# Padded column tables, whole-height spectral weight transfers, and one w2 block loaded earlier

## The chip, the cores and the metric

The kernel runs on one core of a Trainium2 chip. The core has a matrix engine (PE, with its weight loads listed as PEld), a vector engine (DVE), a scalar engine (ACT), GpSimd (POOL), a sync engine (SP) that here only issues transfers, and 16 DMA engines that move the data. The metric is the device time of one launch in microseconds; lower is better.

## The reference

One forward and backward pass of two blocks on an input of 2048 rows by 448 columns (bf16). Block A is a spectral filter: layer norm, a two-dimensional real FFT, a product with complex weights `w_r + i w_i` of shape 2048 x 225, the inverse FFT, and a residual. Block B is an MLP across the 2048 rows with a hidden width of 1792, after two layer norms, and another residual.

```python
def _A_ref(x, w_r, w_i):
    X = rfft2(x.astype(float32))
    X = X * (w_r + 1j * w_i)
    return irfft2(X, s=(S, D)).astype(bfloat16)

def _B_ref(x, w1, b1, w2, b2):
    h = _layernorm(x)
    u = gelu(einsum("bsd,sf->bdf", h, w1) + b1)
    return transpose(einsum("bdf,fs->bds", u, w2) + b2, 0, 2, 1)

h  = x + _A_ref(_layernorm(x), A_w_r, A_w_i)
h2 = h + _B_ref(_layernorm(h), B_w1, B_b1, B_w2, B_b2)
```

The outputs are `h2` and the gradients of x, w_r, w_i, w1, b1, w2 and b2 for a given `grad_out`.

## The kernel before

Everything is written as a list of operations which a planner (`Plan`, L141) puts in an order before the program is built. It holds a cost for each operation, a priority that follows the longest chain behind it, and rings of buffers; each engine then executes its own list strictly in that order. Transfers issued by SP keep the order in which the code names them (`place`, L471). Loads and tables go through SP (`ld` L482, `ld_parts` L547); stores go through POOL (`st` L488). A transfer that SP issues also waits until the one issued eight places earlier has landed, because the program gives SP's transfers eight semaphores in turn.

The FFT is done with matmuls. `fft_rows` (L704) folds the normed rows on DVE into the tile `w`, multiplies with the table `kf` into the bank kind `sp`, and evicts into `zt`. `fft_cols` (L743) takes 16 column steps. `step1` multiplies `zt` with the table `df`, which has 113 rows (DC), and DVE combines the two halves into `gg` (L766, two operations a step). `step2` multiplies `gg` with the table `hf` into `xs` (forward) or `ds` (backward). `cmul` (L800) is the complex product with the spectral weights on DVE: two products `t_r` and `t_i` (L809), then a sum and a difference (L816, L818), for five groups of column steps. Both L809 operations read the weights' tile as a whole, so they wait for both its parts. `ifft_cols` and `ifft_rows` go back with the tables `hi`, `di` and `kinv`.

The spectral weights are read twice from DRAM by `ld_w` (L563): into `w_t` for the forward pass and into `w_b` for the backward pass. SBUF partition 64 b + q holds the 16 weight rows from 32 q + 16 b on, 3,600 numbers or 7,200 bytes in one piece. `ld_w` moves each of the real and the imaginary part in two transfers, one for b = 0 and one for b = 1, of 64 partitions each.

The MLP's products fill the PE between these steps. `ps_mg` is grad_out times w2: 14 blocks of w2, each loaded with a transposing transfer by `ld_w2T` (L554) into the five-slot ring `w4`. `ps_mm` are the products with w1, w2 and later grad_out times g (gradient of w2), and `ps_mw` is the gradient of w1. The gradients of the spectral weights are five groups of DVE products into the tile `gw`, each stored by four POOL transfers of 64 partitions (L1222).

SP's order at the start is: the four parts of x, `kf`, the first w2 block and the two parts of `go_n` among them; then `df1`, `hf`, two w2 blocks, `w_t` in four transfers, `hi`, the fourth w2 block, `kinv`, `di0`, `ident`, `b1r`, `b2r`, and further w2 blocks. In the backward pass it is: the transposed grad_out (`goT`), `df0`, `w_b` in four transfers, `di1`, three parts of x again (`xr`), and the transposed `hlnT` and `du_t`.

Of the kernel before, what the change touches and what calls it, by code (L numbers as in the profile page):

```python
# [18 lines left out]
P = 128  # L19
S = 2048  # L20
D = 448
DF = 225
# [3 lines left out]
NJ = 16  # L26
DC = 113
# [10 lines left out]
def _tables():  # L38


    tb = {}
    q = np.arange(P)
    t_q, pl_q = q // 4, q % 4
    same = (pl_q[:, None] == np.arange(4)[None, :]).astype(np.float64)
    kf = np.zeros((P, 32, 4))
    ke = np.zeros((32, 4, P))
    ko = np.zeros((32, 4, P))
    for j in range(16):
        al = 2 * np.pi * (t_q * j % 32) / 32
        c, s = np.cos(al), np.sin(al) if j else -np.cos(np.pi * t_q)  # L50
        kf[:, 2 * j, :] = c[:, None] * same
        kf[:, 2 * j + 1, :] = -s[:, None] * same
        ke[2 * j] = c[None, :] * same.T
        ke[2 * j + 1] = -s[None, :] * same.T
        ko[2 * j] = -c[None, :] * same.T
        ko[2 * j + 1] = (-s if j else s)[None, :] * same.T
    tb["kf"] = _bf(kf.reshape(P, P))
    tb["kinv"] = _bf(np.stack([ke.reshape(P, P), ko.reshape(P, P), -ko.reshape(P, P)], 1))
    k2 = np.arange(DF)

    def dtab(scale):

        t = np.zeros((DC, 6, DC))
        ke_, ko_ = np.arange(0, DF, 2), np.arange(1, DF, 2)
        d = 112 - np.arange(DC)
        th = lambda k: 2 * np.pi * (d[:, None] * k[None, :] % D) / D
        twice = np.where(d == 112, 0.5, 1.0)[:, None]
        for i, (f, k) in enumerate(((np.cos, ke_), (np.cos, ko_), (np.sin, ke_), (np.sin, ko_))):
            t[:, i, 0:len(k)] = twice * f(th(k)) * scale[k]
        t[:, 4:6] = -t[:, 2:4]  # L70
        return t

    wt = np.full(DF, 2.0 / (S * D))
    wt[[0, DF - 1]] = 1.0 / (S * D)
    tb["df1"] = _bf(dtab(wt))
    tb["df0"] = _bf(dtab(np.ones(DF)))

    def itab(w):
        a = np.zeros((P, 2, DF))
        b = np.zeros((P, 2, DF))  # L80
        d = np.arange(DF)
        for c in range(2):
            kk = np.arange(P) + 97 * c
            th = 2 * np.pi * (kk[:, None] * d[None, :] % D) / D
            a[:, c] = np.cos(th) * w[kk][:, None]
            b[:, c] = np.sin(th) * w[kk][:, None]
        a[: 128 - 97, 1] = 0
        b[: 128 - 97, 1] = 0
        return np.stack([a, b], 1)

    tb["di0"] = _bf(itab(np.ones(DF)))
    wc = wt.copy()
    wc[0] = 0
    tb["di1"] = _bf(itab(wc))

    pp = np.arange(64)
    p = 16 * (pp % 4) + pp // 4
    qq = np.arange(64)
    hf = np.zeros((P, NJ + 1, 2, 2, 64))
    hi = np.zeros((P, NJ, 2, 64))  # L100
    lo, up = slice(0, 64), slice(64, 128)
    th = lambda r: 2 * np.pi * (p[:, None] * (32 * qq[None, :] + r) % S) / S
    for j in range(NJ):
        for b in range(2):
            hi[(lo, up)[b], j, 0], hi[(lo, up)[b], j, 1] = np.cos(th(j + 16 * b)).T, np.sin(th(j + 16 * b)).T
        if j:
            c, s = np.cos(th(j)), np.sin(th(j))
            hf[lo, j, 0, 0], hf[up, j, 0, 0], hf[lo, j, 0, 1], hf[up, j, 0, 1] = c, s, -s, c
            c, s = np.cos(th(32 - j)), np.sin(th(32 - j))
            hf[lo, j, 1, 0], hf[up, j, 1, 0], hf[lo, j, 1, 1], hf[up, j, 1, 1] = c, -s, -s, -c  # L110
    c, s = np.cos(th(0)), np.sin(th(0))
    hf[lo, 0, 0, 0], hf[lo, 0, 0, 1], hf[up, 16, 0, 0], hf[up, 16, 0, 1] = c, -s, s, c
    c, s = np.cos(th(16)), np.sin(th(16))
    hf[up, 0, 1, 0], hf[up, 0, 1, 1], hf[lo, 16, 1, 0], hf[lo, 16, 1, 1] = c, -s, -s, -c
    tb["hf"], tb["hi"] = _bf(hf), _bf(hi)
    tb["ident"] = _bf(np.eye(P))
    return tb
# [280 lines left out]
def kernel(  # L398
# [159 lines left out]
    def table(name, ringname, shape):  # L558
        t = const2(ringname, shape, name)
        ld(t, lambda b: b[:], hnd[name].ap(), int(np.prod(shape)) * 2)  # L560
        return t

    def ld_w(dst):  # L563
        for c, src in enumerate((A_w_r, A_w_i)):
            v = src.rearrange("(q b r) k -> b q r k", b=2, r=NJ)
            for b_ in range(2):
                ld_parts(dst, [(c, b_)], lambda b, c=c, b_=b_: b[64 * b_:64 * b_ + 64, c], v[b_], 64 * NJ * DF * 2)

    ld_x(0)
    kf = const("kf", [P, 5, P])  # L570
# [4 lines left out]
    ld_x(2)  # L575
    ld_go(8, 16)
    ld_x(3)
    df1 = table("df1", "df", [DC, 6, DC])
    hf = table("hf", "hf", [P, NJ + 1, 2, 2, 64])
    ld_w2T(1)  # L580
    ld_w2T(2)
    w_t = big(4, [P, 2, NJ, DF], "w_t")
    ld_w(w_t)
    hi = const("hi", [P, NJ, 3, 64])
    ld(hi, lambda b: b[:, :, 1:3, :], hnd["hi"].ap(), P * NJ * 2 * 64 * 2, w=(hi, 0))
    ld_w2T(3)
    kinv = table("kinv", "kinv", [P, 3, P])
    di0 = table("di0", "di", [P, 2, 2, DF])
    ident = table("ident", "ident", [P, P])
# [153 lines left out]
    def fft_cols(zt, dtab, dst):  # L743


        G = {}

        def step1(j):
            pr = bank("sp", [P, 4, DC])
            calls = []  # L750
            for k, c in ((0, 0), (1, 2), (2, 1), (3, 3)):
                for half, rows_ in ((0, LO), (1, UP)):
                    plane = 2 * j + (half if k < 2 else 1 - half)
                    t = k if k < 2 else k + 2 * half
                    calls.append((DC, lambda k=k, rows_=rows_, pr=pr: pr[rows_, k, :],
                                  lambda c=c, plane=plane: zt[:, c, plane, :], lambda t=t: dtab[:, t, :], True, True))
            matmuls(pr, calls, [zt, dtab], mm(*[DC] * 4), "cols")
            g_ = G[j] = k1([P, 2, 2 * DC], "gg")
            if j == 0:
                copy(evict(452), lambda: g_[:].rearrange("p s (k t) -> p s t k", t=2),  # L760
                     lambda: pr[:].rearrange("p (s t) k -> p s t k", t=2), [pr], [g_])
                return
            b = pl.buf("f2", [P, 2, DC], "gb", F32)
            copy(on_act(226), lambda: b[:], lambda: pr[:, 2:4, :], [pr], [b])
            for s_, op in ((0, ALU.add), (1, ALU.subtract)):
                pl.op(on_dve(226), lambda e, on, s_=s_, op=op: e.tensor_tensor(  # L766
                    out=g_[:, s_, :].rearrange("p (k t) -> p t k", t=2), in0=pr[:, 0:2, :], in1=b[:], op=op),
                    r=[pr, b], w=[(g_, s_)])

        def step2(j):  # L770
            px = bank("sp", [P, 2, DF])
            calls = []
            for im in range(2):
                if j == 0:
                    terms = [[(0, 0, 0), (0, 16, 1)], [(0, 0, 0), (0, 16, 1)]]
                else:
                    terms = [[(j, j, 0)], [(16 - j, 16 - j, 1)]]
                for n in range(len(terms[0])):
                    for half, rows_ in ((0, LO), (1, UP)):
                        gj, ti, s_ = terms[half][n]  # L780
                        calls.append((DF, lambda im=im, rows_=rows_, px=px: px[rows_, im, :],
                                      lambda ti=ti, half=half, im=im: hf[:, ti, half, im, :],
                                      lambda gj=gj, s_=s_: G[gj][:, s_, 0:DF], n == 0, n == len(terms[0]) - 1))
            rd = [G[0]] if j == 0 else [(G[j], 0), (G[16 - j], 1)]
            matmuls(px, calls, rd + [hf], mm(*[DF] * (len(calls) // 2)), "cols")
            copy(evict(450), lambda: dst[:, :, j, :], lambda: px[:], [px], [(dst, j)])

        step1(8)
        step2(8)
        for a in range(7, 0, -1):  # L790
            step1(a)
            step1(16 - a)
            step2(a)
            step2(16 - a)
        step1(0)
        step2(0)
# [354 lines left out]

    df0 = table("df0", "df", [DC, 6, DC])
    w_b = big(0, [P, 2, NJ, DF], "w_b")
    ld_w(w_b)
    di1 = table("di1", "di", [P, 2, 2, DF])
# [52 lines left out]
    for j0, j1 in JG:  # L1210
        cur = []

        def out(a, b, cur=cur):
            t = pl.buf("e4", [P, 2, b - a, DF], "gw")
            cur.append(t)
            return ((lambda: t[:, 0]), (lambda: t[:, 1])), lambda c: [(t, c)]

        cmul(ds, xs, out, j0, j1, True)
        t = cur[0]
        for c in range(2):  # L1220
            for b_ in range(2):
                st(o23[c][b_, :, j0:j1, :], lambda t=t, c=c, b_=b_: t[64 * b_:64 * b_ + 64, c],  # L1222
                   64 * (j1 - j0) * DF * 2, [(t, c)])

    LO, UP = slice(0, 64), slice(64, 128)
    last = None
# [73 lines left out]
```

## Time and profile before

| what | value |
|---|---|
| time, median of 3 runs | 363.59 us (363.09 to 381.46) |
| the profiled execution: its own time | 366.62 us |
| its span, first to last instruction | 364.8 us |
| PE busy | 333.0 us (91%) |
| DVE busy | 273.2 us (75%) |
| ACT busy | 192.5 us (53%) |
| POOL busy | 59.6 us (16%) |
| bytes moved by DMA | 80.67 MB, mean 221 GB/s |
| SP's DMA queue, share of 16 engines | 71.0% |

Times inside the profile count from the span's first instruction. "Busy" counts the time in which an engine executes; a wait's row names who waited, for what, how long in total, how many times, and the longest. A chain or timeline row gives the start, the length and the instruction. In the DMA views the window is cut in 40 equal slices: the row GB/s says what all engines together moved in each slice.

### The profile page before, as it was taken

The numbers are of one execution on the slowest core, as the hardware profiler recorded it, in microseconds if no ns is written. First come the engines' busy times: TensorE is split into PE (matmuls) and PEld (weight loads), VectorE is DVE, ScalarE is ACT, GpSimd is POOL, SyncE is SP. The second block draws the span as 40 slices with busy tenths as digits, with TensorE's granted clock in tenths as the row PEclk, the third lists the DMA queues.
The fourth block names the chain that finished last, engine by engine and source line by source line (L and its number), as shares of the span: only waits on it lengthen the run. The fifth ranks groups of instructions, "written<-read, shape, count | busy, mean of one in ns | idle before, by whom it ended". The sixth has DMA issues, their size and how long they took to land.

```text
span 364.8 us, 6559 instructions
## 1 busy us (share of the span) xinstructions
PE 333.0 (91%) x2411; PEld 180.7 (50%) x2411; DVE 273.2 (75%) x705; ACT 192.5 (53%) x387; POOL 59.6 (16%) x107
## 2 busy tenths in 40 slices
PE   0538799999999999999999999899999999999994
PEld 0224445577655555545555555555455765434441
DVE  5993869979738999252225978889999999977442
ACT  1372554438638777210237232589787899434332
POOL 0000000002210111032210200011111444545221
PEclk9976989999999999999999999999999999999999
DMA  7999997999899999299999999999996574554553
GB/s 173 329 145 223 197 183 154 268 203 239 265 318 275 326 263 305 98 291 292 198 280 235 249 230 204 215 109 215 205 190 221 175 246 174 202 203 179 212 203 152
DMA packets 138192, 80.67 MB, mean 221 GB/s; under 512 B 98318, under 2 KB 130928, under 8 KB 138032
## 3 DMA queue, kind: packets, MB, share of 16 engines
q1 hardware_dynamic: 130672, 52.67, 71.0%
q0 software_dynamic: 7488, 27.58, 21.5%
q8 instruction: 19, 0.31, 0.4%
q14 instruction: 13, 0.11, 0.1%
HBM read 30.12 MB, written 27.08 MB: 157 GB/s over the span
## 4 chain that ended last, share of the span: by engine, by line
PE 75%; DVE 9%; SPq 8%; DMA 4%; ACT 2%; issue 1%; POOLq 0%; ACTq 0%
PE ps_mm L505 40%; PE ps_sp L505 13%; PE ps_mw L505 12%; PE ps_mg L505 10%; SPq L482 7%; DMA w2T<-in_B_w_dram 4%; DVE junk L1126 2%; DVE junk L1110 2%; SPq L547 2%; DVE w L719 1%; ACT v L1119 1%; DVE u L719 1%; DVE go_r L1129 1%; DVE w L497 0%; DVE nm L1116 0%
## 5 line engine op out<-in xcount | busy, mean ns | idle before, releaser
L505 PE MATMUL ps_mg<-go_n,w2T 128*128 128x448 bf16 x224 | 53.0, 374 | 19.9 <-DMA go_n<-in_grad_out_dram 13.3
L505 PE MATMUL ps_mm<-goT,g_t 128*128 128x512 bf16 x224 | 55.6, 380 | 0.5 <-ACT v L1119 0.5
L505 PE MATMUL ps_mw<-du_t,hlnT 128*128 128x448 bf16 (+1 forms) x256 | 44.9, 353 | 0.0
L505 PE MATMUL ps_mm<-gT,w2c 128*128 128x448 bf16 x224 | 42.9, 352 | 0.5 <-DVE gT L1008 0.5
L505 PE MATMUL ps_mm<-du,w1T 128*128 128x449 bf16 x224 | 43.1, 353 | 0.0
L505 PE MATMUL ps_mm<-hln,w1c 128*128 128x448 bf16 x224 | 42.7, 352 | 0.0
L505 PEld LDWEIGHTS <-w2T 128*128 128x128 bf16 x224 | 20.8, 101 | 38.9 <-DMA w2T<-in_B_w_dram 16.1
L495 ACT CAST s<-ps_mw 128x448 bf16<-128x448 f32 x36 | 18.0, 535 | 29.8 <-PE ps_mw L505 26.3
L505 PEld LDWEIGHTS <-hlnT 128*128 128x128 bf16 (+1 forms) x256 | 20.3, 97 | 24.5 <-issue 7.6
L505 PEld LDWEIGHTS <-w2c 128*128 128x128 bf16 x224 | 21.9, 98 | 21.1 <-issue 0.7
L505 PEld LDWEIGHTS <-w1T 128*128 128x128 bf16 x224 | 21.8, 97 | 21.1
L505 PEld LDWEIGHTS <-w1c 128*128 128x128 bf16 x224 | 21.9, 98 | 20.5
L505 PEld LDWEIGHTS <-g_t 128*128 128x128 bf16 x224 | 19.8, 97 | 21.0 <-issue 3.6
L497 DVE CAST s<-ps_mw 128x448 bf16<-128x448 f32 x28 | 17.1, 622 | 17.3 <-PE ps_mw L505 11.2
L1094 DVE SCALAR_TENSOR_TENSOR h<-ps_mm,b2c,hr 128x448 bf16<-128x448 f32 x16 | 9.9, 678 | 23.2 <-PE ps_mm L505 22.9
L488 POOL DMA_DIRECT2D out_dram<-s x30 | 16.4, 548 | 65.7 <-ACT s L495 36.3
L1119 ACT ACTIVATE v<-ps_mm,nm,rstd_h 128x448 f32<-128x448 f32 x16 | 11.6, 724 | 26.9 <-DVE nm L1116 24.5
L495 ACT CAST s<-ps_mm 128x512 bf16<-128x512 f32 x38 | 22.7, 600 | 4.7 <-PE ps_mm L505 4.4
L1101 ACT ACTIVATE gb2j<-go_r 128x448 bf16<-128x448 bf16 x16 | 9.2, 574 | 28.2 <-DMA go_r<-in_grad_out_dram 27.8
L766 DVE TENSOR_TENSOR gg<-ps_sp,gb 128x226 bf16<-128x226 f32 x60 | 20.6, 410 | 2.6 <-ACT gb L495 2.6
L495 ACT CAST eo<-ps_sp 128x450 bf16<-128x450 f32 x31 | 16.4, 554 | 5.1 <-PE ps_sp L505 5.1
L495 ACT CAST zt<-ps_sp 113x512 bf16<-113x512 f32 x27 | 13.8, 603 | 8.2 <-PE ps_sp L505 8.1
(122 smaller groups left out, 552.5 us busy)
## 6 DMA issues: line engine op xcount, KB each, us to landing
w2c<-in_B_w_dram SPq DMA_DIRECT2D x8, 896.0 KB, 8.3
out_dram<-s POOLq DMA_DIRECT2D x14, 512.0 KB, 3.9
out_dram<-s POOLq DMA_DIRECT2D x16, 448.0 KB, 2.8
w1c<-in_B_w_dram SPq DMA_DIRECT2D x6, 1024.0 KB, 10.7
x<-in_A_x_dram SPq DMA_DIRECT2D x4, 448.0 KB, 7.0
go_n<-in_grad_out_dram SPq DMA_DIRECT2D x2, 896.0 KB, 7.1
hn_d<-x POOLq DMA_DIRECT2D x4, 448.0 KB, 5.9
hln_d<-hln POOLq DMA_DIRECT2D x4, 448.0 KB, 4.2
```

Source lines behind the costliest of these rows:

```text
L482: e.dma_start(out=out(dst), in_=in_() if callable(in_) else in_, **kw)
L488: e.dma_start(out=out() if callable(out) else out, in_=in_())
L495: e.copy(out=out(), in_=in_())
L497: e.tensor_copy(out=out(), in_=in_())
L505: e.matmul(out(), lhsT=lhsT(), rhs=rhs(), start=start, stop=stop)
L547: e.dma_start(out=out(dst), in_=in_() if callable(in_) else in_, **kw)
L719: pl.op(tt(4 * n), lambda e, on: e.tensor_tensor(out=out(), in0=in0(), in1=in1(), op=op), r=r, w=w_)
L766: pl.op(on_dve(226), lambda e, on, s_=s_, op=op: e.tensor_tensor(out=g_[:, s_, :].rearrange("p (k t) -> p t k", t=2), in0=pr[:, 0:2, :], i ...
L1094: pl.op(on_dve(448), lambda e, on, t=t, p2=p2, h2=h2: e.scalar_tensor_tensor(out=h2[:], in0=p2[:, 0:D], scalar=b2c[:, t:t + 1], in1=hr[t / ...
L1101: pl.op([("ACT", 0.55, 0.65)], lambda e, on, h=h: e.activation(out=gb2j[:], in_=go_r[:, h, :], func=ACT.Copy, accum_out=gb2[:, h:h + 1]), ...
L1110: pl.op([("DVE", 0.69, 0.77)], lambda e, on: e.tensor_tensor_reduce(out=junk[:], in0=pb[:, 0:D], in1=xhat(), scale=nm.rneg[:, h:h + 1], sc ...
L1119: pl.op([("ACT", 0.6, 0.7)], lambda e, on: e.activation(out=v[:], in_=pb[:, 0:D], func=ACT.Identity, scale=nm.rstd[:, h:h + 1], bias=nm1[: ...
```

## The change

Four edits:

- The tables `df1` and `df0` get 128 rows in place of 113; the added rows are zeros and are not read, since the matmul takes rows 0 to 112.
- `ld_w` moves each part of the spectral weights in one transfer of 128 partitions. The DRAM side is written as `b q (r k)`: an outer index b of 2 (step 3,600 numbers), then q of 64 (step 7,200), then 3,600 numbers in one piece. The SBUF side has 128 partitions.
- The spectral gradients are stored in the same form: two POOL transfers a group in place of four, 10 in all in place of 20.
- The fourth w2 block is loaded ahead of `w_t` instead of behind `hi`.

```diff
     def dtab(scale):
-        t = np.zeros((DC, 6, DC))
+        t = np.zeros((P, 6, DC))
...
-            t[:, i, 0:len(k)] = twice * f(th(k)) * scale[k]
+            t[0:DC, i, 0:len(k)] = twice * f(th(k)) * scale[k]
...
     def ld_w(dst):
         for c, src in enumerate((A_w_r, A_w_i)):
-            v = src.rearrange("(q b r) k -> b q r k", b=2, r=NJ)
-            for b_ in range(2):
-                ld_parts(dst, [(c, b_)], lambda b, c=c, b_=b_: b[64 * b_:64 * b_ + 64, c], v[b_], 64 * NJ * DF * 2)
+            ld_parts(dst, [c], lambda b, c=c: b[:, c].rearrange("p r k -> p (r k)"),
+                     src.rearrange("(q b r) k -> b q (r k)", b=2, r=NJ), P * NJ * DF * 2)
...
-    df1 = table("df1", "df", [DC, 6, DC])
+    df1 = table("df1", "df", [P, 6, DC])
     hf = table("hf", "hf", [P, NJ + 1, 2, 2, 64])
     ld_w2T(1)
     ld_w2T(2)
+    ld_w2T(3)
     w_t = big(4, [P, 2, NJ, DF], "w_t")
     ld_w(w_t)
     hi = const("hi", [P, NJ, 3, 64])
     ld(hi, lambda b: b[:, :, 1:3, :], hnd["hi"].ap(), P * NJ * 2 * 64 * 2, w=(hi, 0))
-    ld_w2T(3)
...
-                                  lambda c=c, plane=plane: zt[:, c, plane, :], lambda t=t: dtab[:, t, :], True, True))
+                                  lambda c=c, plane=plane: zt[:, c, plane, :], lambda t=t: dtab[0:DC, t, :], True, True))
...
-    df0 = table("df0", "df", [DC, 6, DC])
+    df0 = table("df0", "df", [P, 6, DC])
...
         for c in range(2):
-            for b_ in range(2):
-                st(o23[c][b_, :, j0:j1, :], lambda t=t, c=c, b_=b_: t[64 * b_:64 * b_ + 64, c],
-                   64 * (j1 - j0) * DF * 2, [(t, c)])
+            st(o23[c][:, :, j0:j1, :].rearrange("b q r k -> b q (r k)"),
+               lambda t=t, c=c: t[:, c].rearrange("p r k -> p (r k)"), P * (j1 - j0) * DF * 2, [(t, c)])
```

The sizes given to the planner change with the transfers, so it also writes a somewhat different order for every engine. Around the first read of the weights, PE's new list takes up the fourth w2 block's product between the column steps, and DVE's new list has 17 `gg` operations ahead of the first `t_r` (12 before). In the backward pass the two orders are the same up to the first products with `w_b`.

## The prediction

> **What bounds the kernel now.** I read first the busy times by stage: from 46.4 us to 359 us PE has hardly an idle microsecond (64.40 of 64.40 in 246.6 to 311, 48.00 of 48.00 in 311 to 359), so any time that PE loses in the middle is lost for good. DVE is nearly full up to 311 as well:
>
> ```profile
> 246.60:311.00 64.40, 64.40 (x577) 36.95 (x572) 63.20 (x149) 56.55 (x112) 16.20 (x30) 1.00 0.87 205
> 311.00:359.00 48.00, 48.00 (x272) 21.33 (x271) 30.91 (x54) 18.09 (x37) 19.39 (x36) 1.00 0.53 194
> ```
>
> (Columns: stretch, length, busy us of PE, PEld, DVE, ACT, POOL, granted clock, DMA share, GB/s.) Idle PE time lies before 46.4. Who PE waits for in 0 to 60 us:
>
> ```profile
> PE ps_mg L505 <- DMA w2T<-in_B_w_dram: 6.6, 2, 3.5
> ```
>
> These are a wait of 3.5 us for the second w2 block (PE goes on at 29.15) and one of 3.1 us for the fourth (46.44). SP's list tells why:
>
> ```profile
> 10.53 5.55 SPq L482 DMA_DIRECT2D hf<-tab_hf  x1
> 16.12 12.55 SPq L482 DMA_TRANSPOSE w2T<-in_B_w_dram  x2
> 28.71 1.23 SPq L547 DMA_DIRECT2D w_t<-in_A_w_r_dram  x2
> ...
> 31.92 10.97 SPq L482 DMA_TRANSPOSE w2T<-in_B_w_dram  x1
> ```
>
> A transposing transfer behind copies sits in its issue until those have drained (10.97 us behind `w_t` and `hi`). What drains slowly the DMA view of 0 to 50 us shows, in slices of 1.25 us:
>
> ```profile
> GB/s 0 86 315 292 155 205 156 277 358 406 354 343 375 175 349 366 193 29 23 28 23 245 159 255 230 248 207 236 219 225 192 168 214 145 194 219 198 22 109 284
> ```
>
> In slices 17 to 20 (21.3 to 26.3 us) the 16 engines move 23 to 29 GB/s. Two views inside it say what that is:
>
> ```profile
> DMA packets 44, 0.05 MB, mean 25 GB/s; under 512 B 13, under 2 KB 44, under 8 KB 44
> ...
> DMA packets 7, 0.06 MB, mean 23 GB/s; under 512 B 0, under 2 KB 0, under 8 KB 0
> GB/s 0 0 0 0 0 131 0 0 0 0 131 0 0 0 0 131 0 0 0 0 131 0 0 0 0 131 0 0 0 0 131 0 0 0 0 131 0 0 0 0
> ```
>
> The first is 21.6 to 23.4: rows of `df1` (1,356 bytes), one after another. The other two are 23.45 to 26.1: rows of `hf` (8,704 bytes), one every five slices of 66 ns, 0.331 us each. So the 113-row table went through one DMA engine alone, and the `hf` rows of that engine queued behind it while the rest had nothing to do. Transfers with 128 or 64 rows do use all: `w_t` in four 64-row transfers ran at 213 GB/s:
>
> ```profile
> DMA packets 710, 1.92 MB, mean 213 GB/s; under 512 B 457, under 2 KB 457, under 8 KB 710
> ```
>
> **How I read that.** 113 is prime and got one engine; 64 and 128 got the full width. I take it that a transfer is shared out evenly by its outermost index, on as many engines as divide it. Then the padded table gains and the new read of the weights loses: its DRAM side now leads with b = 2. No row shows such a transfer; the bounds are one engine (as `df1`) and 16 (as `w_t`). I take two, nearest to the `df1` row, the only one with a leading count that 16 doesn't divide.
>
> The Trainium skill (DMA: Bandwidth & Descriptors, "Why a DMA increments its semaphore by 16 and not by 1") states such a rule: the largest number up to 16 that divides the slowest dimension over one on both sides. By that rule 113 rows get one engine, the trace agrees (23 GB/s), and 2 against 128 gets two; no run here shows the latter yet.
>
> **The sum, part by part.**
>
> *Padded tables.* The other engines were done with `hf` near 20.5 us (193 GB/s in the slice that ends at 21.3, 29 after it). With 128 rows `df1`'s 0.17 MB take some 0.5 us at 350 GB/s and `hf` ends near 20.9 in place of 26.1. The second w2 block comes 5.2 us earlier, at about 23.9, and PE, free of `kf` work at 25.64, doesn't wait: the 3.5 us go. The fourth block is issued right behind the third, so the 3.1 us go too: -6.6 us, if nothing else stopped PE. In the backward pass `df0` isn't waited for by PE now; its gain there is nothing.
>
> *First whole-height read, `w_t`.* SP issues it after three w2 blocks (issue 2.2 us each where nothing holds it): 21.2 + 2.2 + 2.2 = 25.6; it starts when they are through, about 27.5. Two engines carry 128 rows of 7,200 bytes each; by the `hf` row of one engine 7,200 / 8,704 x 0.331 = 0.274 us, so 35.1 us: done at 62.6, landed about 63.5. DVE wants it early: `t_r` stands behind 17 `gg` and ahead of the rest. Before:
>
> ```profile
> 41.54 1.08 DVE L809 TENSOR_TENSOR t_r<-xs,w_t 128x1800 bf16<-128x1800 bf16 x1
> 42.54 1.09 DVE L809 TENSOR_TENSOR t_i<-xs,w_t 128x1800 bf16<-128x1800 bf16 x1
> ```
>
> Queued behind `t_r` on DVE is the 18th `gg`. PE's `step2` of column step 4 needs it, and PE takes its list in order, so PE stops near 42.5 us with six matmuls of the fourth w2 block done, until 63.5 + 1.08 + 1.09 + 0.3 = 66.0. That is the state that PE has now at 48.5 (six such matmuls and the `hf` steps after them: 46.44 + 2.01). So **+17.5 us, in which the -6.6 is already spent**. PE's granted clock was 0.50 in 26.4 to 32.0, around its idle time; PE would come back at half clock for a little: +0.5. Further w2 blocks queue behind `w_t`, `hi`, `kinv`, `di0` (some 3 us), then 3 us from drain to landing (26.1 to 29.1 now): about 69, and PE gets to the fifth block after 71. Together **+18**.
>
> *Second read, `w_b`.* Times as now; all is shifted by the 18. It starts near 225.7 behind `goT`; 35.1 us on two engines end near 261, plus one or two stores of 512 KB on the same engines (1.2 us of each engine) and landing: about 263, and `xr` right behind it. DVE wants `xr` at 246.62 and `w_b` at
>
> ```profile
> 247.25 1.10 DVE L809 TENSOR_TENSOR t_r<-ds,w_b 128x1800 bf16<-128x1800 bf16 x1 [0.25 <-ACT ds L495]
> ```
>
> so DVE stands about 16.5 us. PE has cover until about 252 (22 matmuls with `goT`, whose banks DVE partly evicts) and then stands too. DVE is 98% busy from there to 311, so its delay isn't made up: **+16.5**. `hlnT` and `du_t` come later with it, but are wanted only at 311.
>
> *Stores.* POOL issues 10 transfers fewer (0.53 us each); POOL is idle more than half of that stage, so 0. On two engines a store of 173 KB takes 64 rows x 1,350 bytes at the `hf` rate, 3.3 us against 2.8 us to landing now; the tile is wanted again some 6 us later. Uncovered it would be 0 to 1 us a group; I take 0.
>
> Sum: 18 + 16.5 = +34.5 us. On the profiled execution's 366.62 that is 401; on the median of 363.59, **398 us**. A run within 2% (7.3 us) can't be told from no change.
>
> **The rivals.**
>
> *1, not slower: the read uses all 16 engines.* The point that decides is whether the SBUF side's 128 or the DRAM side's 2 sets the width. For it: every transfer of 128 partitions in the trace has full width; against it: none of them has a small outer index. Then `w_t` takes 16 rows an engine at 0.274 to 0.54 us, at most the 8.7 us of now (1.84 MB at 213 GB/s), and only the -6.6 is left: 357 us, 1.8% faster. The Trainium skill (same page, "Rules for kernel authors") recommends this outcome's form, one 128-partition transfer in place of two halves. Chance 0.11.
>
> *2, the read is slower still.* `w_t` rows now take about 0.54 us of an engine (256 rows in 8.7 us on 16). If that price belongs to the rows and not to the crowding of all engines on 64 partitions, or if one engine gets it all, a read takes 69 or 70 us: +34 or +35 twice, 466 to 468 us. Against it: a lone engine kept 0.331 us for longer rows. Chance 0.07.
>
> *3, the second stall is hidden.* If PE's `goT` products ran on without DVE, only the +18 counts: 382. Against it: fixed orders and DVE at 98%. Chance 0.12.
>
> **How the numbers follow.** The forecast, 385 to 420, has 0.70: its upper end takes a row at the `df1` rate (31 rows in 1.8 us, so 0.31 us for 7,200 bytes: +4.4 us a read), some 3 us more of half clock at each stall, and more stores beside the second read; its lower end, cover of 6 us for each stall. The range 376 to 424 takes in rival 3 and leaves out rivals 1 and 2 (0.18). Rival 1 lies at the edge of 2%: faster 0.05, same 0.06; slower 0.89.
>
> **What would show it.** Right: in the changed kernel's DMA view about 50 GB/s for some 35 us from 27 us on, and again in the backward pass; `t_r` on `w_t` near 63; PE idle from about 42 to 66 and again some 15 us before the first product with `w_b`; the second w2 block's product near 25.6 with no wait for it. Wrong: over 200 GB/s during `w_t` (rival 1), a load of 70 us (rival 2), or a PE that doesn't stand in the backward pass (rival 3). A `gg` or bank that PE needs sooner than I read in the order would lengthen the first stall by little, since its end is set by the load.

## The result, and the profile after

The changed kernel takes 1.175 times as long as before (95% interval 1.159 to 1.191), some 64 us more. The undisturbed runs, which alone enter the ratios, are 425.66 and 428.27 us, and the profiled execution is a disturbed one of 434.45 us (span 432.7), so its marks come a few us late (2 to 4 us for the second to fourth mark, against `e_inplace` below). The forecast was slower, 398 us; the range ended at 424.

The direction and both stalls came as foreseen; a third loss was not. The marks of the two traces show where the time went:

| mark | before | after | shift |
|---|---|---|---|
| first matmul with the second w2 block | 29.15 | 25.38 | -3.8 |
| PE: first product with `w1c` | 104.31 | 129.75 | +25.4 |
| PE: first product with `w1T` | 189.70 | 215.14 | +25.4 |
| PE: first gradient of w1 (`ps_mw`) | 311.39 | 358.51 | +47.1 |
| last PE instruction ends | 359.50 | 426.46 | +67.0 |

The forecast had +18 for the second and third mark and +34.5 for the last two. PE's waits of the whole span of the changed kernel (who waited for what: us in total, times, longest) name all three losses:

```profile
PE ps_sp L505 <- DVE gg L765: 25.0, 1, 25.0
PE ps_mm L505 <- ACT s L495: 18.2, 1, 18.2
PE ps_mg L505 <- DMA go_n<-in_grad_out_dram: 13.3, 2, 12.6
PE ps_mw L505 <- DVE s L497: 12.7, 4, 5.4
PE ps_sp L505 <- DVE w L497: 5.6, 3, 4.6
PE ps_mg L505 <- DMA w2T<-in_B_w_dram: 3.5, 1, 3.5
```

The third and fifth were there before. The first is the stall at the first read, the second the one at the second read, the fourth is new, and the last is a w2 block at 121.6 us.

**First read.** The DMA view of 0 to 50 us no longer has the slices of 23 to 29 GB/s near 21 to 26 us; from 28.75 us on it has slices of about 52 instead. The second line is the window 27 to 65.5 us:

```profile
GB/s 0 66 351 346 152 272 142 316 354 389 358 359 387 423 420 177 157 108 268 267 206 169 6 46 52 58 65 52 52 58 52 65 52 52 58 125 224 133 52 46
...
DMA packets 2230, 2.38 MB, mean 62 GB/s; under 512 B 1972, under 2 KB 1972, under 8 KB 2227
```

DVE's rows (start, length, idle time before; its L808 is L809 of the kernel before) show what this did:

```profile
48.76 1.10 DVE L808 TENSOR_TENSOR t_r<-xs,w_t 128x1800 bf16<-128x1800 bf16 x1 [9.22 <-DMA w_t<-in_A_w_r_dram]
66.16 1.10 DVE L808 TENSOR_TENSOR t_i<-xs,w_t 128x1800 bf16<-128x1800 bf16 x1 [16.31 <-DMA w_t<-in_A_w_i_dram]
```

The kernel's description above says that both operations wait for both parts. The rows say otherwise: `t_r` went as soon as the real part had landed. `t_i` had to wait for the imaginary part, and that sets the end.

**Second read.** DVE waits for `xr`, which SP had issued behind `w_b`; the weights themselves are there by then:

```profile
291.61 0.40 DVE L693 TENSOR_SCALAR xr<-xr,rstd_x,nb_x 128x448 bf16<-128x448 bf16 x1 [19.95 <-DMA xr<-in_A_x_dram]
291.92 1.09 DVE L808 TENSOR_TENSOR t_r<-ds,w_b 128x1800 bf16<-128x1800 bf16 x1
```

**The clock behind each stall.** The table of stretches (columns: stretch, length, busy us of PE, PEld, DVE, ACT, POOL, granted clock, DMA share, GB/s) has each stall and the time behind it, and then the last stage:

```profile
42.64:67.64 25.00, 0.00 (x0) 0.00 (x0) 2.58 (x4) 0.67 (x1) 0.00 (x0) 0.58 0.27 74
67.64:73.80 6.16, 6.16 (x48) 2.81 (x48) 4.25 (x9) 2.18 (x5) 0.00 (x0) 0.50 0.85 193
275.40:293.60 18.20, 0.00 (x0) 0.00 (x0) 1.99 (x3) 1.93 (x4) 0.00 (x0) 0.59 0.96 81
293.60:299.10 5.50, 5.50 (x20) 1.87 (x19) 5.21 (x13) 3.41 (x7) 0.53 (x1) 0.50 1.28 230
358.50:426.50 68.00, 55.20 (x271) 23.24 (x269) 29.75 (x53) 19.00 (x39) 18.93 (x29) 0.87 0.46 142
```

PE is busy behind both stalls, but for 6.16 and 5.50 us at half clock: about 3 us of work are lost each time. In the last stage, which had 48.00 of 48.00 us before, PE now stands 12.8 of 68.00 us. Its busy time there also grew, from 48.0 to 55.2 us, at a mean granted clock of 0.87 (1.00 before).

**Stores.** DVE's rows of the gradients' tile in that last stage, and below them how long its stores took (from the view of the tile):

```profile
371.93 0.52 DVE L815 TENSOR_TENSOR gw<-t_r,t_i 128x675 bf16<-128x675 bf16 x1 [5.58 <-DMA out_dram<-gw]
...
383.45 0.52 DVE L815 TENSOR_TENSOR gw<-t_r,t_i 128x675 bf16<-128x675 bf16 x1 [6.79 <-DMA out_dram<-gw]
...
396.09 0.52 DVE L815 TENSOR_TENSOR gw<-t_r,t_i 128x675 bf16<-128x675 bf16 x1 [8.44 <-DMA out_dram<-gw]
```

```profile
DMA to landing us min/median/max: 6.4/8.1/10.9
```

Before, landing took 2.0/2.6/4.6 us. Each group uses all three slots of the ring `e4` (`t_r`, `t_i`, `gw`), so the next group's `gw` cannot be written until the group before has landed: the groups come 11 to 13 us apart (5 to 7 before). The evictions of `ps_mw` that DVE has queued behind `gw` wait with it, and PE for their banks.

### The profile page after: what moved, and what is told of

It reads as the page before. It is cut to its first block, busy times and chain, and to the rows that moved or that the text cites. A ratio compares the mean times of both kernels' runs of the same rounds, so it can differ in the third digit from the quotient of the medians.

```text
span 432.7 us, 6538 instructions
## 1 busy us (share of the span) xinstructions
PE 346.4 (80%) x2411; PEld 184.8 (43%) x2411; DVE 271.1 (63%) x702; ACT 194.0 (45%) x390; POOL 57.4 (13%) x97
## 4 chain that ended last, share of the span: by engine, by line
PE 53%; DMA 25%; DVE 10%; SPq 6%; ACT 3%; issue 2%; POOL 0%; DVEq 0%; ACTq 0%
PE ps_mm L505 32%; PE ps_sp L505 10%; DMA w_t<-in_A_w_i_dram 9%; DMA out_dram<-gw 9%; PE ps_mg L505 8%; DMA xr<-in_A_x_dram 5%; SPq L482 5%; PE ps_mw L505 4%; DVE junk L1109 2%; DMA w2T<-in_B_w_dram 2%; DVE junk L1125 2%; ACT v L1118 1%; SPq L547 1%; DVE w L718 1%; DVE u L718 1%
## 5 line engine op out<-in xcount | busy, mean ns | idle before, releaser
L505 PE MATMUL ps_mm<-goT,g_t 128*128 128x512 bf16 x224 | 58.4, 393 | 18.2 <-ACT s L495 18.2
L505 PE MATMUL ps_mg<-go_n,w2T 128*128 128x448 bf16 x224 | 54.6, 386 | 17.1 <-DMA go_n<-in_grad_out_dram 13.3
L505 PE MATMUL ps_mw<-du_t,hlnT 128*128 128x448 bf16 (+1 forms) x256 | 52.1, 396 | 12.7 <-DVE s L497 12.7
L505 PE MATMUL ps_mm<-gT,w2c 128*128 128x448 bf16 x224 | 42.9, 352 | 0.5 <-DVE gT L1007 0.5
L505 PEld LDWEIGHTS <-hlnT 128*128 128x128 bf16 (+1 forms) x256 | 22.0, 105 | 42.7 <-issue 28.3
L495 ACT CAST s<-ps_mw 128x448 bf16<-128x448 f32 x35 | 17.5, 535 | 47.6 <-PE ps_mw L505 38.7
L505 PE MATMUL ps_sp<-gg,hf 128*64 128x225 bf16 x136 | 11.2, 274 | 25.0 <-DVE gg L765 25.0
L495 ACT CAST s<-ps_mm 128x512 bf16<-128x512 f32 x43 | 25.4, 594 | 9.4 <-PE ps_mm L505 9.2
L815 DVE TENSOR_TENSOR gw<-t_r,t_i 128x675 bf16<-128x675 bf16 (+1 forms) x5 | 2.7, 536 | 27.6 <-DMA out_dram<-gw 27.6
```

Of the source, the lines that this page charges most:

```text
L495: e.copy(out=out(), in_=in_())
L505: e.matmul(out(), lhsT=lhsT(), rhs=rhs(), start=start, stop=stop)
```

## The experiments

Ratios are to the kernel before, run beside each; times in the text are a ratio's excess times 364 us.

| kernel | ratio (95%) | us |
|---|---|---|
| changed kernel | 1.1751 (1.1593 to 1.1909) | +64 |
| e_oldstores | 1.1128 (1.1061 to 1.1195) | +41 |
| e_oldread | 1.0311 (1.0259 to 1.0364) | +11 |
| e_inplace | 1.1473 (1.1353 to 1.1593) | +54 |
| e_first | 1.0586 (1.0511 to 1.0662) | +21 |
| e_second | 1.0499 (1.0393 to 1.0606) | +18 |
| e_best | 0.9988 (0.9958 to 1.0017) | 0 |
| e_noearly | 0.9838 (0.9792 to 0.9884) | -6 |
| e_early | 1.0041 (0.9987 to 1.0094) | +1.5 |
| e_w2first | 0.9821 (0.9779 to 0.9862) | -6.5 |
| e_lead128 | 0.9948 (0.9912 to 0.9984) | -2 |
| e_lead84, one run | 376.77 us (before: 365.3) | +11 |
| e_div, one run | 361.13 us (before: 365.5) | -4 |

### Are the stores a loss of their own?

`e_oldstores` takes the changed kernel and puts the old stores back; `e_oldread` puts the old reads back and keeps the new stores.

```diff
 # e_oldstores
-            st(o23[c][:, :, j0:j1, :].rearrange("b q r k -> b q (r k)"), ...)
+            for b_ in range(2):
+                st(o23[c][b_, :, j0:j1, :], lambda t=t, c=c, b_=b_: t[64 * b_:64 * b_ + 64, c], ...)
 # e_oldread
-            ld_parts(dst, [c], lambda b, c=c: b[:, c].rearrange("p r k -> p (r k)"), ...)
+            v = src.rearrange("(q b r) k -> b q r k", b=2, r=NJ)
+            for b_ in range(2):
+                ld_parts(dst, [(c, b_)], lambda b, c=c, b_=b_: b[64 * b_:64 * b_ + 64, c], v[b_], ...)
```

> The changed kernel with the gradients stored in four half-height transfers a group again; reads and tables stay changed. Theory: the whole-height stores cost the last 20 us of the loss (the tile gw waits for its own slow store, 8.1 us to landing where it was 2.6), so the time falls from 427 to about 407, the landing is 2.5 to 3 us again, and PE's last stage (first gradient of w1 to the end) is as long as before the change, some 50 us. Rival, as the prediction had it: the stores cost nothing and the last stage is longer because the late reads push other work into it; then the time stays within 3 us of 427.

> The changed kernel with both reads of the weights in four half-height transfers again; tables, w2 block and whole-height stores stay changed. Theory: both PE stalls go (25 and 18 us with their half clock, 54 us with the 6.6 that the tables save), so 427 falls to about 373, that is 357 plus some 16 to 20 for the stores. Rival: the stores hurt only because everything behind the late second read comes bunched; then the time is near 357.

Measured: +41 and +11. The stores are worth 64 - 41 = 23 us beside the late reads, and the on-record "0" falls. In `e_oldstores` PE's last stage, from the first gradient of w1 to PE's end, takes 47.5 us, as expected (48.1 before, 67.9 in the changed kernel), and the gradients' stores land as they did before:

```profile
DMA to landing us min/median/max: 2.3/2.6/3.4
```

By themselves the stores cost 11. The changed kernel and `e_oldread` order DVE's list differently: in `e_oldread`, as before the change, the first group of gradients comes early (277.9 us), and only the other four follow one another, 10 to 11 us apart. DVE's waits for a store there:

```profile
DVE gw L816 <- DMA out_dram<-gw: 16.8, 3, 5.7
```

That is three waits, where the changed kernel, with all five groups in the last stage, has four and 27.6 us. So the rival of `e_oldread`, that the stores hurt only because work comes bunched behind the late read, holds for part of the price: 11 of the 23 us are there without it.

### What do slow stores hold up?

`e_inplace` keeps the changed kernel's slow stores, but the products are written over `xs`, so that no slot is waited for.

```diff
         def out(a, b):
-            t = pl.buf("e4", [P, 2, b - a, DF], "gw")
-            ...
+            return (((lambda: xs[:, 0, a:b, :]), (lambda: xs[:, 1, a:b, :])),
+                    lambda c: [(xs, j) for j in range(a, b)])
```

> The changed kernel, its slow whole-height stores kept, but the gradients are written over xs (no longer needed by then) in place of a tile of the three-slot ring e4, so that no product on DVE waits for a store. Theory: the whole price of the stores beside the late reads is this wait (DVE stood 27.6 us for stores, four times), so the time is that of the run with half-height stores, 406 to 409, with stores that still take 8 us to land. Rival: the slow stores hold up the end through the queue or POOL's longer issue (0.83 us in place of 0.53); then the time stays above 420.

Measured: +54, between the two theories. The slot's wait is worth some 10 of the 23 us. PE's last stage is 55.7 us here, against 67.9 in the changed kernel and 47.5 in `e_oldstores`. What is left shows in this kernel's waits of 350 to 420 us:

```profile
ACT s L495 <- DMA out_dram<-s: 18.4, 5, 7.0
...
DVE s L497 <- DMA out_dram<-s: 14.8, 4, 6.3
...
PE ps_mw L505 <- ACT s L495: 4.5, 3, 3.4
```

The evictions now wait for the stores of the w1 gradient, and PE for their banks; behind the longest of these waits (378.7 to 390.6 us) its granted clock is 0.86. A store of `s` with 448 KB lands after 6.2 us (median; 2.8 in `e_oldstores`), the gradients' own with 168.8 KB after 13.5:

```profile
out_dram<-s POOLq DMA_DIRECT2D x16, 448.0 KB, 6.2
...
out_dram<-xs POOLq DMA_DIRECT2D x8, 168.8 KB, 13.5
```

Which engines the stores share shows in the trace's semaphore events: a store's semaphore gets 16 increments. In the changed kernel, of the store that POOL issues at 374.30 us, 14 come after 2.5 to 2.9 us and two later, at 380.79 and 382.05. So two engines carry its data. Of the group's second store, issued at 375.14, 12 come after 3.4 to 4.7 us, two at 381.17 and 382.41, right behind the first store's two, and the last two at 382.93 and 383.33. So the second store is on two other engines; the four other groups look the same. A store is 32 packets of 5,400 bytes at 0.223 us (median), 3.6 us on two engines. The rest of its landing is not the time of its data: in `e_lead128` (below) a store of the same size goes to 16 engines, and lands after 2.9 us all the same.

```profile
DMA to landing us min/median/max: 2.7/2.9/3.1
```

The stores of `s` behind the gradients are late in two ways. Of the one issued at 400.86 us, 14 increments come after 4.9 to 5.7 us and the last two after 7.5 and 8.2; in `e_oldstores` all 16 of the one issued at 381.48 come after 2.6 to 2.8. That the last two wait behind the gradients' rows is how I read it. Why the other 14 are late as well the trace doesn't show.

### What sets the width of a transfer?

`e_lead128` keeps one transfer a part for reads and stores, but lets the DRAM side lead with 128. `e_lead84` has old stores, and reads that lead with 8 (first) and 4 (second). `e_div` is the kernel before with tables of 116 (forward) and 120 rows (backward).

```diff
 # e_lead128, in ld_w (the stores likewise)
-                     src.rearrange("(q b r) k -> b q (r k)", b=2, r=NJ), P * NJ * DF * 2)
+                     src.rearrange("(p r) k -> p (r k)", r=NJ), P * NJ * DF * 2)
 # e_lead84
+                     src.rearrange("(q b r) k -> b q (r k)", b=lead, r=NJ), P * NJ * DF * 2)
+    ld_w(w_t, 8)
+    ld_w(w_b, 4)
 # e_div
-    df1 = table("df1", "df", [DC, 6, DC])
+    df1 = table("df1", "df", [116, 6, DC])
-    df0 = table("df0", "df", [DC, 6, DC])
+    df0 = table("df0", "df", [120, 6, DC])
```

> The changed kernel, reads and stores still whole-height in one transfer each, but the DRAM side leads with an index of 128 (the rows of the weights and of their gradients are then taken and put in another order, so the weights' rows stand against other rows of the spectrum; the work is the same). Theory: the leading 2 alone made them slow; with 128 a read takes 9 to 10 us on 16 engines at 200 GB/s or more, a store lands in 2 to 3 us, and the time is that of the tables and the w2 block alone, about 357. Rival: one transfer of 128 rows of 7,200 bytes is slow by itself (long rows, or one semaphore count): then a read takes 35 us again and the time stays near 427.

> Padded tables and earlier w2 block, half-height stores; both reads in one transfer a part, the DRAM side led by an index of 8 in the first read and of 4 in the second (the weights' rows then stand against other rows of the spectrum; the work is the same). Theory, as many engines as divide the leading number: 8 engines, 32 rows each at 0.274 us, some 9 us and 210 GB/s for the first; 4 engines, 64 rows each, 17.5 us and 105 GB/s for the second. So the first read costs little or nothing and the second a few us at most: 364 to 369. Rival, a leading index that is not 128 falls to two engines whatever it is: 35 us each, and about 409 as with both reads whole-height.

> The kernel before with 116 rows in the forward table (df1) and 120 in the backward one (df0) in place of 113; added rows are zeros. Theory, the largest number up to 16 that divides the rows: 4 engines for 116, 15 for 120. So 29 rows of 60 to 120 ns stand one after another on each of 4 engines, df1 is through 1.7 to 3.5 us after its start (7.2 with 113 rows, 2.2 with 128) and the last rows of hf end by about 22 us (26.1 with 113, 20.3 with 128); df0 is through in about 1 us if nothing else is on the engines. Rival, only numbers that 16 divides are shared out: then 116 behaves as 113, over 7 us, and hf ends at 26.

Both kernels with other leading indices, `e_lead128` and `e_lead84`, take the weights' rows in another order, so they do not compute the reference; the transfers have the same size and the work is the same.

The trace's semaphore events count the engines. The semaphore of a narrow transfer makes one jump near its issue (none where 16 increments follow), and later single increments as the data lands:

| transfer | leading counts (DRAM, SBUF) | late increments | median us of a 7,200-byte row | all 256 rows, us |
|---|---|---|---|---|
| `df1` before | 113, 113 | 1 | | |
| `df1` in e_div | 116, 116 | 4 | | |
| `df0` in e_div | 120, 120 | 15 | | |
| `w_t` after | 2, 128 | 2 | 0.274 | 38.7 |
| `w_b` in e_lead84 | 4, 128 | 4 | 0.334 | 27.3 |
| `w_t` in e_lead84 | 8, 128 | 8 | 0.548 | 19.0 |
| `w_t` in e_lead128 | 128, 128 | 16 | 0.273 | 6.0 |
| `w_t` before, four transfers | 64, 64 | 16 each | 0.534 | 9.1 |

So the leading 2 alone made the read slow: with 128 in front the same transfer takes 6.0 us, the stores land after 2.9 us, and the whole kernel is 2 us under the one before (357 us was expected). The DMA view of 26.7 to 32.8 us in `e_lead128`:

```profile
DMA packets 1187, 2.08 MB, mean 341 GB/s; under 512 B 930, under 2 KB 930, under 8 KB 1186
```

`e_div` agrees: `df1` is through 3.8 us after its first row, and `hf`'s last row ends at 22.4 us (26.1 before), a little over what was expected. `hf`'s rows cost 0.46 us there (median; 0.33 before).

The Trainium skill (DMA: Bandwidth & Descriptors, "Why a DMA increments its semaphore by 16 and not by 1") says that k engines are used, the largest number up to 16 that divides the slowest dimension of both sides, and that the semaphore jumps to 16 - k at once. Every row of the table agrees.

The number of engines is not the whole price. Eight engines took 19 us where 9 were expected, since a row cost 0.548 us in place of 0.274. The second read, on four, took 27.3 us where 17.5 were expected. PE stands 6.2 us at the first and 6.0 us at the second, and the time is 377 us instead of 364 to 369. The four half-height transfers of the kernel before pay the same double price on 16 engines. The Trainium skill has a rule for the latter (SBUF — State Buffer, "Door 1: The DMA port swizzle (why `[64,N]` ≈ `[32,N]`)"): 64 consecutive partitions reach only half of SBUF's ports. The measured 0.534 against 0.273 us agrees. By the same map, partitions 32 apart share a port; with a leading 8 and one chunk of 16 partitions to an engine, engines in step would meet in pairs, which would fit 0.548. With a leading 4 they would meet too, and there the row took only 0.334. The trace does not tell which engine moved a row, so this stays open.

### How much is each read?

`e_first` and `e_second` have padded tables, the earlier block and old stores, with one read whole-height and the other in halves.

```diff
-    def ld_w(dst):
+    def ld_w(dst, whole):
...
-    ld_w(w_t)
+    ld_w(w_t, True)     # e_first; False in e_second
...
-    ld_w(w_b)
+    ld_w(w_b, False)    # e_first; True in e_second
```

> Padded tables and earlier w2 block, half-height stores, and only the first read (w_t) whole-height. By the prediction's terms: 18 above the kernel before, about 382 to 383. By the trace of the changed kernel: 25.4 above, about 389 to 390, because PE comes back at half clock and waits later for a w2 block.

> Padded tables and earlier w2 block, half-height stores, and only the second read (w_b) whole-height. The tables and the block alone gave nothing (364.9), so by the prediction's term the time is 16.5 above, about 381; by the trace of the changed kernel 21.7 above, about 386 to 387. Rival: without the late first read the second one starts in front of other traffic and is covered by PE's work with grad_out (the prediction's third rival): below 375.

Measured: +21 and +18; both together (`e_oldstores`) +41. The first read lies between the two expectations: PE stands 26.1 us for `gg`, as in the changed kernel, but waits only 1.0 us for a later w2 block, not 3.5. The second read lies between its two as well, nearer to the prediction's; its stall is there without the first read (PE waits 16.0 us for ACT's `s`), so the third rival falls.

### Where did the 6.6 us of the tables go?

`e_best` is the change without its reads and stores, `e_noearly` the padded tables alone, `e_early` the earlier block alone. `e_w2first` is `e_best` with the last two w2 blocks ahead of the second set of w1 columns:

```diff
 # e_w2first
     for j in range(10, 12):
         ld_w2T(j)
-    ld_w1(4, 4, 7)
     for j in range(12, 14):
         ld_w2T(j)
...
+    ld_w1(4, 4, 7)
     ld_w1(5, 7, 11)
```

> Only the padded tables and the earlier w2 block; reads and stores in half-height transfers as before. Theory: the waits of 3.5 and 3.1 us for w2 blocks go and nothing takes their place: 357 us, 0.98 of before. Rival: another wait takes their place (w_t comes 2 us later, DVE stands for it at 41.5), and 2 to 4 us of the gain are left: 360 to 362.

> The kernel before with the padded tables alone; the fourth w2 block stays behind the weights and hi. By the prediction's terms the tables save 3.5 us by themselves (360); by the run with tables and block, which gave 0 since the later w2 blocks become the bound, the same time as before: 363 to 366.

> Padded tables and earlier w2 block with half-height reads and stores (365 us, no gain), and the last two w2 blocks loaded ahead of the second set of w1 columns (1.5 MB) in SP's order. Theory: the 5 us that PE had gained at 57 us were lost again at 91 to 95 us, where it waited 1.0 and 3.0 us for these two blocks behind that copy and then ran 4 us at half clock; with the blocks first, 4 to 6 us come back: 359 to 361 us, 0.985 of before. Rival: the DMA engines are full from 60 to 97 us (83 to 92% of the time), so what is moved ahead only makes the w1 columns late, which PE wants at 103: 364 to 366.

> The kernel before with the fourth w2 block ahead of the weights alone; tables of 113 rows. By the prediction's terms this edit saves the wait of 3.1 us for the fourth block: 360 to 361. By the runs so far (tables alone 359.2, tables and block 364.9) the edit costs some 5 to 6 us where the tables are padded, since the last w2 blocks then come behind the w1 copy; if it costs the same without them, 368 to 371; if that loss needs PE to be early, 361 to 365.

The tables alone save 6 us, more than the 3.5 of the prediction's terms, and not the nothing that had been read out of `e_best`. With the earlier block nothing is left, where 357 or 360 to 362 was expected. The tables remove both waits by themselves: in `e_noearly` the fourth block's issue ends at 36.6 us (42.9 before), and PE stands for no w2 block at all; it only waits 1.4 us for `hi`. PE's rows of `e_best` around 91 us show where the gain goes:

```profile
91.62 0.55 PE L505 MATMUL ps_mg<-go_n,w2T 128*128 128x448 bf16 x2 [0.98 <-DMA w2T<-in_B_w_dram]
95.14 6.78 PE L505 MATMUL ps_mg<-go_n,w2T 128*128 128x448 bf16 x26 [2.97 <-DMA w2T<-in_B_w_dram]
```

PE waits 4.0 us for the last two blocks, and its granted clock is 0.88 on average over 91 to 105. SP's rows (start, length of issue) of `e_best`, then of `e_noearly`, tell why:

```profile
72.82 3.96 SPq L547 DMA_DIRECT2D w1c<-in_B_w_dram  x2
76.88 14.06 SPq L482 DMA_TRANSPOSE w2T<-in_B_w_dram  x2
```

```profile
69.11 3.19 SPq L547 DMA_DIRECT2D w1c<-in_B_w_dram  x2
72.39 12.47 SPq L482 DMA_TRANSPOSE w2T<-in_B_w_dram  x2
```

The last two blocks stand behind 1.5 MB of w1 columns in both, but with the earlier block they are issued 4.5 us later (the tenth block too: 57.3 against 53.2, after a wait for PE to free a slot). Why PE frees that slot later in the new order stays open. `e_w2first` takes them out from behind that copy, and 6.5 us come back, a little more than expected; no w2 block is waited for any more. It and `e_noearly` are the fastest kernels of this case that compute the reference: 1.6 to 1.8% under the one before. Without the tables, the early block costs 1.5 us (its interval takes in 0) and does not save the 3.1 of the prediction's terms: the wait for the fourth block goes, the one for the second stays (until 28.92), and two come up at the last two blocks (until 94.7 and 98.9, 4.0 us together).

## Why the prediction was wrong

**What bounds the kernel, and the width of the new read: right.** The rule "on as many engines as divide the outermost index" held in every row of the table of widths, the row price taken from `hf` (0.274 us) is the measured one, and PE stood from 42.64 to 67.64 us where 42.5 to 66.0 was forecast. (The forecast put both products behind the landing. In the trace only `t_i` stands there, but the landing came some 2.5 us later.) Rival 1 falls: the DRAM side's 2 sets the width, not SBUF's 128. Its price was wrong too, since the 128-row form gave 0.995 of before and not 357 us. Rivals 2 and 3 fall with the rows of 0.274 us and with `e_second`.

**The sum: one term was missing.** By the runs:

| step | forecast | measured |
|---|---|---|
| tables, earlier block, first read | +18 | +21 (e_first) |
| second read | +16.5 | +20 (e_oldstores less e_first; alone +18) |
| stores | 0 | +23 (changed kernel less e_oldstores) |
| sum | +34.5 | +64 |

The step that failed is "Stores", which ends with "I take 0". Its 3.3 us for a store's data on two engines were nearly right: the packets give 3.6. But it set them beside 2.8 us to landing, and those are hardly data at all: the same store on 16 engines lands after 2.9 us, of which two packets on each engine are about 0.4. With 3.6 us in place of these 0.4 a narrow store lands after some 6 us, an estimate; the trace has 8.1 (median). The step also counted one store where the tile waits for two, issued one behind the other, of which the second lands after 8.1 to 10.9 us. Against the "some 6 us" until the tile is wanted again, that is late in every group. The step looked only for who wants the tile: the stores of `s`, which come late behind the gradients, are about half of the price by `e_inplace`. And it took the order of the kernel before for the gradients, where the changed list has all five groups in the last stage.

**The stalls were sized some 3 us short each.** The step gave the half clock 0.5 us at the first stall and nothing at the second; 6.16 and 5.50 us at 0.50 cost about half of that. Each read also took longer than the 35.1 us of the sum, 38.7 and 38.0 us from its first row to its last. The range's upper end had "some 3 us more of half clock at each stall", so this alone would have stayed inside it.

**The -6.6 was half right.** Both waits went (25.38, and no wait for the fourth block). But the tables alone bring 6 us of it, not 3.5, and with the earlier block the gain is spent at the last w2 blocks. The step asked what is late next only as far as the first read. In the sum it did no harm, since the first stall had already used the gain up.

## What to carry to other kernels

By the table of widths a transfer runs on as many engines, up to 16, as divide its leading counts on both sides, so two half-height transfers that lead with 64 can beat one of full height that leads with 2, and a table of 113 rows is worth padding; read both sides of each pattern in the order in which it is written, for stores as well as for loads. When a store narrows, put the longer time of its data on top of the landing that it has now, not in its place; count every store that the buffer waits for, and ask who else's stores stand behind it. An earlier place in a load queue is paid for by what then comes later in it: look for the next transfer behind the move that PE will stand for, all the way to the end of that stream.

## What the runs showed of the hardware that was not expected

The rows of a 128-partition read cost 0.273 us on 16 engines at once, as little as on two; those of 64-partition transfers cost 0.534, so the four halves of the kernel before need 9.1 us for what one transfer of 128 leading rows does in 6.0. Eight engines at 0.548 us a row moved 97 GB/s (1.84 MB in 19.0 us), not twice what four did (68 GB/s at 0.334). A whole-height store that leads with 2 also costs POOL more to issue: 0.83 us against 0.53 for a half-height one and 0.54 for one that leads with 128. Two such stores one behind the other were on different pairs of engines, and the stores behind them came late on all 16.
